# Third chunk: heads 4 to 7 first, transposed by DMA; later landing times for queries and keys in the plan; new priorities

## The chip, the cores and the metric

The kernel runs on one core of a Trainium2 chip. The metric is the device time of one execution in microseconds (us). Nine executions are given by their median. One more execution was recorded by the hardware profiler, and every row of a profile below comes from that one.

## The reference

An attention layer is followed by a gated feed-forward layer. Attention has 4 batches, 8 heads, 768 positions and 64 dimensions per head. Heads 0, 2 and 6 are "retrieval" heads with the full causal mask. The other five are "streaming" heads: a query sees the first 4 positions (the sinks) and the last 64.

```python
scores = scale * np.matmul(q, k.transpose(0, 1, 3, 2))
mask   = causal                                   # heads 0, 2, 6
mask   = causal & (pos_k < 4 | (q - k) < 64)      # the others
a      = softmax(np.where(mask, scores, -1e9))
x      = np.matmul(a, v)        # to [3072 tokens, 512]

g, val = x @ w_gate, x @ w_val  # 512 -> 1536
ffn    = (gelu(g) * val) @ w_out
out    = x + sigmoid(x @ w_res) * ffn
```

## The kernel before, in words

The 3072 tokens are cut into six chunks of 512 tokens (`CHUNKS`, numbered 0 to 5; each is four tiles of 128 tokens, and chunk 2, the third, is batch 1, tiles 2 to 5). A chunk goes through attention, then the gate and value products (L1111, twelve feature blocks `f`, each with 4 matmuls for the gate and 4 for the value), then the residual gate (L1141) and the output product (L1156). Attention of chunk c+1 is woven into the output products of chunk c.

Heads are worked in four pairs, `PAIRS = ((0, 2), (4, 6), (1, 3), (5, 7))`. A chunk runs over the pairs in `ORDER = (0, 2, 1, 3)` or in `LATER = (1, 3, 0, 2)`. `ORDER` takes heads 0, 2, 1, 3 first; `LATER` takes heads 4, 6, 5, 7 first. For each pair there are scores (L852), exponentials on ScalarE (L868), a mask on VectorE (L904), the products with the values (L976, L986, L1000), and a division (L1041, L1043). Sink scores are at L943. The normalised rows, in 16 bits, sit in `x16`; the feed-forward products need them with features on partitions, in `xT`. That transposition has two forms:

- `to_features`: TensorE transposes (L1065, four per feature block), then a copy out of PSUM on VectorE or ScalarE (L1072), one for each of the pair's two feature blocks.
- `to_features_dma`: one DMA transpose issued by SyncE (L1056) for both feature blocks.

Which form is used is decided in `attention`:

```python
if c >= DT_FIRST and P.p == order[1]:
    to_features_dma(c, P.heads[0] // 2, P.pr, x16, xdeps, xtbuf, xttoks)
```

and the order of the pairs by `order = ORDER if c < DT_FIRST else LATER`. So `DT_FIRST` sets both.

Queries and keys of chunks 0 and 1 are loaded as rows (`loads_rows`) and transposed on TensorE (L676). From chunk 2 on, `loads_natural` loads each tile in two halves (L553, issued by GpSimd, which also converts to 16 bits), and SyncE issues a DMA transpose for each tile (L717, `dT`) into `qkt`. When all eight tiles of a segment are there, SyncE issues a copy of one head's half to other partitions (L725, `q6`), which part of the scores of pair (4, 6) reads.

No order is written out by hand. Every piece of work is a `Task` with an engine, a planned duration and a priority. `Graph.schedule` plays the tasks through in planned time, and each engine's instructions are then emitted in the order that this plan gave. `Task.late` adds to the planned landing time of a DMA. It reaches no instruction by itself. `HINTS` replaces the priorities of single tasks, by task number. While TensorE has nothing to do at the start, the plan fills it with matmuls on a blank tile (L1173). On the chip each engine and each queue goes strictly through its own list, and waits are semaphores.

Of the kernel before, what the change touches and what calls it, by code (L numbers as in the profile page):

```python
# [36 lines left out]

LATER = (1, 3, 0, 2)
ROWS_UNTIL = 2
DT_FIRST = 3  # L40
DT_ALL = 9

VK = ((1, 4), (3, 4), (4, 5), (4, 7))


HINTS = (
    "0:598.78 2:-98.96 3:-24.27 16:511.03 398:-226.32 399:-81.95 400:-169.98 401:-133.18 406:592.76 "
    "428:669.65 590:-107.97 595:554.03 604:-62.97 609:119.02 611:508 631:-103.87 632:500.02 635:591.25 "
    "640:113.91 642:197.51 643:485.34 648:497.6 649:608.77 687:-2618.72 693:998.98 695:-156.54 696:-101.5 "
    "699:-194.37 703:460.62 704:468.99 706:91.16 707:1.21 708:-184.02 711:-2906.86 712:108.67 715:-113.61 "  # L50
    "722:-93.98 726:593.8 732:539.67 737:-3080.99 740:2426.17 743:-43.63 744:44.98 750:-84.74 755:-61.77 "
    "756:-226.32 757:-68.07 758:-100.39 762:-75.67 767:1467.66 783:2538.51 789:1088.69 791:2362.89 "
    "794:489.79 834:-1953.13 885:2499.66 897:2409.44 903:1361.62 910:1573 915:1075.62 921:1094.44 "
    "927:1527.46 933:2646.2 934:3345.41 946:3583 960:3450.9 963:1467.39 982:1981.84 984:1548.12 1014:3374.09 "
    "1025:2486.39 1037:3491.83 1060:2046.57 1061:2453.27 1067:3409.97 1068:1990.02 1069:3494.45 1076:2552.54 "
    "1081:2446.96 1082:3477.51 1099:2162.67 1105:3505.94 1111:3490.47 1117:3067.67 1144:3026.33 1146:3134.85 "
    "1150:118.46 1155:3543.75 1198:3516.67 1304:980.83 1313:4066.75 1341:4517.9 1343:4508.61 1358:985.12 "
    "1363:4003.98 1364:4417.91 1375:5441.35 1388:4117.01 1418:5399.99 1424:4517.89 1429:3494.32 1435:5479.84 "
    "1436:5423.25 1563:5565.33 1567:6542.91 1598:5535.71 1608:2079.98 1609:4991.07 1610:5503.31 1622:2043.57 "
    "1623:5529.25 1628:5543.06 1629:5543.02 1635:6420.01 1659:7430.01 1672:7417.77 1684:7455.84 "  # L60
)

class Task:
# [396 lines left out]
def build_kernel(nc, q, k, v, w_gate, w_val, w_out, w_res, out):  # L460
    assert N_SINK <= 64 and WINDOW == 64
    G = Graph(nc)
# [16 lines left out]
    P_vk = Pool(many("vk", 2, [128, 8, DHEAD + 1], FP16))  # L479
# [21 lines left out]
    def at(buf):  # L501
        if buf.pool is P_ps:
            return psum[:, buf.slot[0] * 512:(buf.slot[-1] + 1) * 512]
        return buf.pool.items[buf.slot]

    def at16(buf):
        return at(buf).bitcast(FP16)
# [17 lines left out]
    t_blank = G.add("dve", 0.1, lambda e: e.memset(blank[:, :], 0.0), [], -99, name="blank")  # L525
# [17 lines left out]
    t_win = t_win0 + [spread(("dve",), 600, m_win[:, 5:7, :], m_win[:, 1:2, :].to_broadcast([128, 2, 128]), 256, t_win),  # L543
                      spread(("dve",), 600, m_win[:, 0, :], m_win[:, 1, :], 128, t_win)]
    for i, vk in enumerate(P_vk.items):
        P_vk.last[i] = [G.add("dve", 0.3, (lambda vk=vk: lambda e: e.memset(vk[:, :, :], 0.0))(), [], -94, name="vzero")]
    for i, va in enumerate(P_v.items):
        P_v.last[i] = [G.add("dve", 0.15, (lambda va=va: lambda e: e.memset(va[:, :, :, DHEAD:DHEAD + 1], 1.0))(),
                             [], -95, name="vones")]

    def dma(eng, prio, cost, out_ap, in_ap, bufs=(), deps=(), name="ld", grp=None):
        issue = 0.85 if eng == "pool" else 1.2
# [93 lines left out]
    def loads_rows(c, si, b, a, z):  # L646

        n = z - a
        BB = batch(b)
        st = Buf(P_st)  # L650
        lo, hi = a * 128, z * 128
        base = {0: -60, 1: -15, 2: 50}[c]
        groups = ((0, 4), (4, 8)) if c == 0 else ((0, 8),)
        tok = {}

        def sv(j, h0, h1, w):
            return at(st)[:, :].rearrange("p (j h w) -> p j h w", j=2, h=NHEAD)[:, j, h0:h1, 0:w]
        for gi, (h0, h1) in enumerate(groups):
            for j, src in enumerate((q, k)):
                t = dma("pool", base + 4 * gi + j, (h1 - h0) * n * 0.089,  # L660
                        (lambda j=j, h0=h0, h1=h1: lambda: sv(j, h0, h1, n * 64))(),
                        src[b, h0:h1, lo:hi, :].rearrange("h (p j) d -> p h (j d)", j=n), bufs=[st])
                for h in range(h0, h1):
                    tok[j, h] = t
        values(b, a, z, base + (10 if c == 0 else 2), False, c == 0)

        per = 1 if c == 0 or n == 4 else 2
        for k_ in range(0, NPAIR, per):
            ps_ = ORDER[k_:k_ + per]
            pr = 1000 * c - 492 + ps_[0] if c else 40 * k_ - 205  # L670
            for js in (((1,), (0,)) if c == 0 else ((0, 1),)):
                scr = Buf(P_ps, "scr" if c else "scr0")
                items = [(p, jj) for jj in js for p in ps_]

                def tr(e, items=items, scr=scr):
                    return [e.transpose(out=at16(scr)[64 * x:64 * x + 64, (m * n + i) * 128:(m * n + i + 1) * 128],  # L676
                                        in_=at(st)[:, (jj * NHEAD + h) * 256 + i * 64:(jj * NHEAD + h) * 256 + (i + 1) * 64],
                                        identity=ident[:, :])
                            for m, (p, jj) in enumerate(items) for i in range(n) for x, h in enumerate(PAIRS[p])]
                tt = G.add("pe", c_mm(128, n) * len(items), tr, [t_ident] + [tok[jj, h] for p, jj in items for h in PAIRS[p]],  # L680
                           pr, bufs=[st, scr], name="qkT")
                tt.mode = "col"


                def ev(on, p0=ps_[0], scr=scr, j0=js[0], m=len(items)):
                    def fn(e):
                        o = at(BB.qkt)[:, :, :, lo:hi].rearrange("c j (y x) w -> c x (j y) w", x=2)[:, p0 % 2]
                        m0 = j0 * 2 + p0 // 2
                        o = o[:, m0:m0 + m, :].rearrange("c m (p j) -> c m p j", j=n)
                        i_ = at16(scr)[:, 0:m * n * 128].rearrange("c (m j p) -> c m p j", m=m, j=n)  # L690
                        return e.tensor_copy(out=o, in_=i_) if on == "dve" else e.activation(out=o, in_=i_, func=AF.Copy)
                    return fn
                w = n * 128 * len(items)
                t = G.flex({"dve": (c_dve(w), ev("dve")), "act": (c_act(w), ev("act"))}, [tt], pr,
                           bufs=[scr, BB.qkt], name="qkE")
                for p, jj in items:
                    for i in range(a, z):
                        (BB.ktok if jj else BB.qtok)[p, i] = t

    def loads_natural(c, si, b, a, z):  # L700

        n = z - a
        BB = batch(b)
        st = Buf(P_st)
        base = -15 if c == 1 else 1000 * (c - 2) + 50
        if BB.q6 is None:
            BB.q6 = Buf(P_q6)
        loaded = []
        for i in range(a, z):
            for j, src in ((1, k), (0, q)):  # L710
                def sv(i=i, j=j):
                    return at(st)[:, (j * 4 + i - a) * 512:(j * 4 + i - a + 1) * 512]
                ds = [dma("pool", base, 0.45,
                          (lambda sv=sv, o=o: lambda: sv().rearrange("p (o h d) -> p o h d", o=2, h=4)[:, o, :, :])(),
                          src[b, :, i * 128:(i + 1) * 128, :].rearrange("(h o) p d -> o p h d", o=2)[o], bufs=[st],
                          grp=("ld", b, i, j)) for o in range(2)]
                t = G.add("sp", 1.65, (lambda sv=sv, i=i, j=j: lambda e: e.dma_start(  # L717
                    at(BB.qkt)[:, j, :, i * 128:(i + 1) * 128], sv(), transpose=True))(), ds, base, bufs=[st, BB.qkt], dma=0.6, name="dT")
                t.late = 3.0
                loaded.append(t)  # L720
                for p in range(NPAIR):
                    (BB.ktok if j else BB.qtok)[p, i] = t
            if i == a:
                values(b, a, z, base, False)
        t = G.add("sp", 0.8, lambda e: e.dma_start(at(BB.q6)[0:64, :, a * 128:z * 128], at(BB.qkt)[64:128, :, 1, a * 128:z * 128]),  # L725
                  loaded, base + 1, bufs=[BB.qkt, BB.q6], dma=0.4, name="q6")
        t.late = 2.0
        for i in range(a, z):
            BB.q6tok[0, i] = BB.q6tok[1, i] = t
# [6 lines left out]
    def attention(c, segs, xbuf, xtbuf, xtoks, xttoks, l0=0, last=(), ek=None):  # L736
# [4 lines left out]
        todo = []  # L741
        order = ORDER if c < DT_FIRST else LATER
        for k_, p in enumerate(order):
# [54 lines left out]
        for P in todo:  # L798
# [4 lines left out]
            if P.heads[0] % 2 == 1:  # L803
                if c >= DT_FIRST and P.p == order[1]:
                    to_features_dma(c, P.heads[0] // 2, P.pr, x16, xdeps, xtbuf, xttoks)
# [467 lines left out]
```

The softmax here doesn't subtract the row's maximum and nothing guards it: scores larger than these inputs give would overflow.

## Time and profile before

| | us |
|---|---|
| median of 9 executions (lowest, highest) | 271.95 (270.97, 272.6) |
| the profiled execution | 271.83 |
| its span in the profile | 270.0 |
| TensorE (PE) busy in the span | 263.7 |
| VectorE (DVE) busy | 141.1 |
| ScalarE (ACT) busy | 139.6 |
| GpSimd (POOL) busy | 87.0 |
| first matmul that is not a filler | 6.05 |
| last matmul ends | 267.1 |

Between the span and the time of the same execution lie 1.83 us. A row of the chain or of a timeline has the start, the length, the engine and the source line. The clock granted to TensorE is 1.00 in every stretch of this profile. A matmul's row tells more by the distance from its start to the next one's start than by its own length, because neighbours overlap.

### The profile page before, as it was taken

How to read it: one execution, taken by the hardware profiler on the slowest of the kernel's cores; microseconds unless marked ns; L12 is line 12 of the kernel's file. 1: busy time of each engine (PE TensorE's matmuls, PEld its weight loads, DVE VectorE, ACT ScalarE, POOL GpSimd, SP SyncE). 2: the span in 40 equal slices, each digit the busy share in tenths (PEclk: the TensorE clock that was granted, in tenths of full speed). 3: DMA queues.
4: the chain of work that ended last, by engine and by line, in shares of the span. 5: the costliest groups of instructions: out<-in, count | busy, mean ns of one | idle time of the engine just before them, and what ended most of it. 6: DMA issues, size and time to landing. Idle time of an engine off the chain costs nothing.

```text
span 270.0 us, 5686 instructions
## 1 busy us (share of the span) xinstructions
PE 263.7 (98%) x2392; PEld 138.6 (51%) x2392; DVE 141.1 (52%) x275; ACT 139.6 (52%) x215; POOL 87.0 (32%) x124
## 2 busy tenths in 40 slices
PE   6999999999999999999999999999999999999995
PEld 5778554465444455444445444455444455444444
DVE  1798235388344456535377533376444376444344
ACT  2685456864235877333884233876333778053300
POOL 8999409995653038992000000000000000000000
DMA  6999999999999999999964100013100015100013
GB/s 82 169 206 207 186 179 229 170 162 172 177 180 148 152 154 215 149 182 169 184 124 117 41 0 0 2 41 94 65 0 0 2 39 80 66 16 0 0 39 119
DMA packets 96506, 29.12 MB, mean 108 GB/s; under 512 B 84448, under 2 KB 92896, under 8 KB 96480
## 3 DMA queue, kind: packets, MB, share of 16 engines
q0 software_dynamic: 70320, 14.69, 65.2%
q1 hardware_dynamic: 26160, 14.07, 27.7%
q8 instruction: 19, 0.31, 0.5%
q14 instruction: 7, 0.06, 0.1%
HBM read 29.36 MB, written 6.29 MB: 132 GB/s over the span
## 4 chain that ended last, share of the span: by engine, by line
PE 85%; DMA 6%; POOL 6%; issue 1%; DVE 1%; POOLq 0%; DVEq 0%
PE ps L1111 41%; PE ps L1156 23%; PE ps L1141 8%; DMA qks<-in_k_dram 6%; PE ps L852 4%; PE ps L986 3%; POOL qks L553 2%; PE ps L976 2%; PE ps L1000 1%; PE ps L1065 1%; POOL va L553 1%; POOL wv L553 1%; PE ps L676 1%; PE ps L943 1%; POOL wg L553 1%
## 5 line engine op out<-in xcount | busy, mean ns | idle before, releaser
L1125 DVE SCALAR_TENSOR_TENSOR hT<-gact,ps 128x512 f16<-128x512 f16 x68 | 45.7, 687 | 62.0 <-ACT gact L1123 34.0
L1123 ACT ACTIVATE gact<-ps 128x512 f16<-128x512 f32 x68 | 40.2, 597 | 73.3 <-PE ps L1111 71.9
L1111 PE MATMUL ps<-xT,wv 128*128 128x512 f16 x272 | 74.6, 380 | 0.0
L1111 PE MATMUL ps<-xT,wg 128*128 128x512 f16 x272 | 74.1, 380 | 0.0
L1156 PE MATMUL ps<-wo,hT 128*128 128x512 f16 (+2 forms) x312 | 70.8, 363 | 0.0
L1111 PEld LDWEIGHTS ps<-xT,wv 128*128 128x128 f16 x272 | 26.3, 98 | 31.2 <-DVE hT L1125 0.4
L1111 PEld LDWEIGHTS ps<-xT,wg 128*128 128x128 f16 x272 | 26.3, 98 | 30.5 <-ACT xT L1072 0.6
L1156 PEld LDWEIGHTS ps<-wo,hT 128*128 128x128 f16 x312 | 27.1, 97 | 26.2 <-issue 0.9
L553 POOL DMA_DIRECT2D qks<-in_k_dram x36 | 28.7, 836 | 32.0 <-DMA qkt<-qks 22.2
L868 ACT ACTIVATE er<-ps 128x1024 f16<-128x1024 f32 (+4 forms) x40 | 34.2, 891 | 7.5 <-PE ps L852 7.3
L553 POOL DMA_DIRECT2D qks<-in_q_dram x36 | 28.8, 849 | 0.8 <-DVE ident L526 0.8
L1160 DVE SCALAR_TENSOR_TENSOR otile<-srs,ps 128x512 f32<-128x512 f32 (+2 forms) x26 | 16.7, 644 | 17.4 <-PE ps L1156 17.2
L1141 PE MATMUL ps<-wr,xT 128*128 128x512 f16 x96 | 24.5, 380 | 0.0
L553 POOL DMA_DIRECT2D va<-in_v_dram x24 | 21.5, 940 | 3.0 <-PE ps L1000 3.0
L1144 ACT ACTIVATE srs<-ps 128x512 f32<-128x512 f32 x24 | 14.3, 597 | 13.6 <-PE ps L1141 13.6
L1163 DVE TENSOR_TENSOR otile<-otile,xtok 128x512 f32<-128x512 f32 (+2 forms) x26 | 16.8, 647 | 0.7
L1043 DVE TENSOR_TENSOR xtok<-ps,rcp 128x512 f32<-128x512 f32 (+1 forms) x28 | 16.9, 609 | 0.5
L852 PE MATMUL ps<-qkt 64*128 64x64 f16 (+3 forms) x391 | 17.0, 213 | 0.1
L852 PEld LDWEIGHTS ps<-qkt 64*128 64x128 f16 x391 | 9.9, 95 | 9.1 <-issue 4.7
L868 ACT ACTIVATE es<-ps 128x1024 f16<-128x1024 f32 (+1 forms) x14 | 12.6, 900 | 3.2 <-PE ps L852 3.2
L1141 PEld LDWEIGHTS ps<-wr,xT 128*128 128x128 f16 x96 | 8.5, 97 | 9.6 <-issue 0.6
L1173 PE MATMUL ps<-blank 128*128 128x128 f16 x109 | 10.8, 248 | 2.6 <-DVE blank L525 2.6
(69 smaller groups left out, 215.4 us busy)
## 6 DMA issues: line engine op xcount, KB each, us to landing
out_dram<-otile SPq DMA_DIRECT2D x23, 256.0 KB, 2.1
va<-in_v_dram POOLq DMA_DIRECT2D x24, 128.0 KB, 18.0
qks<-in_k_dram POOLq DMA_DIRECT2D x32, 64.0 KB, 12.8
qks<-in_q_dram POOLq DMA_DIRECT2D x32, 64.0 KB, 13.2
wg<-in_moe_w_gate_dram POOLq DMA_DIRECT2D x3, 512.0 KB, 10.4
wv<-in_moe_w_val_dram POOLq DMA_DIRECT2D x3, 512.0 KB, 10.8
wo<-in_moe_w_out_dram POOLq DMA_DIRECT2D x4, 384.0 KB, 23.1
vs<-va SPq DMA_DIRECT2D x4, 260.0 KB, 6.7
```

The lines of the kernel that those rows point to most:

```text
L553: return G.add(eng, issue, lambda e: e.dma_start(out_ap(), in_ap), deps, prio, bufs=bufs, dma=cost, name=name, grp=grp)
L852: return [e.matmul(at(scr)[:, oo:oo + w], lhsT=side(BB, low, 1)[half, k0:k0 + 128], rhs=side(BB, low, 0)[half, qq:qq + w], start=True, sto ...
L868: return e.activation(out=o, in_=i_, func=AF.Exp, scale=SM_SCALE)
L1043: t2 = G.add("dve", c_dve(2 * n * 64), lambda e: e.tensor_tensor(out=xview(), in0=avv(0, DHEAD), in1=scale(), op=ALU.mult), [t1] + xdeps, ...
L1111: return lambda e: [e.matmul(at(dst)[:, :], lhsT=w[:, ci, f * 128:(f + 1) * 128], rhs=at(xtbuf)[:, ci, :], start=(ci == 0), stop=(ci == NC ...
L1123: ta = G.add("act", c_act(512), (lambda gb=gb, ga=ga: lambda e: e.activation(out=at(ga)[:, :], in_=at(gb)[:, :], func=AF.Gelu))(), [tg], p ...
L1125: th = G.add("dve", c_dve(512), (lambda vb=vb, ga=ga, f=f: lambda e: e.scalar_tensor_tensor(out=at(h)[:, f, :], in0=at(ga)[:, :], scalar=0 ...
L1141: e.matmul(at(rb)[:, :], lhsT=at(xtbuf)[:, ci, s], rhs=wr[:, ci, :], start=(ci == 0), stop=(ci == NCB - 1))
L1144: ta = G.add("act", c_act(512), (lambda rb=rb, sr=sr: lambda e: e.activation(out=at(sr)[:, :], in_=at(rb)[:, :], func=AF.Tanh, scale=0.5)) ...
L1156: e.matmul(at(fb)[:, w], lhsT=at(h)[:, fi, s], rhs=wo[:, fi, w], start=(fi == 0), stop=(fi == NF - 1))
L1160: t1 = G.add("dve", c_dve(n), (lambda fb=fb, sr=sr, ot=ot, w=w: lambda e: e.scalar_tensor_tensor(out=at(ot)[:, w], in0=at(sr)[:, w], scala ...
L1163: t2 = G.add("dve", c_dve(n), (lambda ot=ot, lt=lt, w=w: lambda e: e.tensor_tensor(out=at(ot)[:, w], in0=at(ot)[:, w], in1=at(xbuf)[:, lt, ...
```

## The change

Four edits, with one new table of priorities.

- `DT_FIRST` goes from 3 to 2. Chunk 2 takes the pairs in the order `LATER`, and its second pair's `x16` (heads 4 to 7) is transposed by one DMA on SyncE instead of by eight TensorE transposes with two copies.
- The planned landing of the row loads of chunk 1 is 1.2 us later (`t.late`), and that of all natural loads of queries and keys 5.0 us later.
- The two kinds of constant fill on VectorE (`vzero`, `vones`) come after the fill of the blank tile.
- `HINTS` is a different table, so that the order of instructions differs on every engine.

```diff
-DT_FIRST = 3
+DT_FIRST = 2
 DT_ALL = 9
...
 HINTS = (
-    "0:598.78 2:-98.96 3:-24.27 16:511.03 398:-226.32 399:-81.95 400:-169.98 401:-133.18 406:592.76 "
...
+    "0:-96.05 3:-32.5 13:-14.98 398:-205.14 399:-3161.01 400:-242.48 401:-60.67 406:194.11 428:585.68 "
...
     for i, vk in enumerate(P_vk.items):
-        P_vk.last[i] = [G.add("dve", 0.3, (lambda vk=vk: lambda e: e.memset(vk[:, :, :], 0.0))(), [], -94, name="vzero")]
+        P_vk.last[i] = [G.add("dve", 0.5, (lambda vk=vk: lambda e: e.memset(vk[:, :, :], 0.0))(), [t_blank], -94, name="vzero")]
     for i, va in enumerate(P_v.items):
         P_v.last[i] = [G.add("dve", 0.15, (lambda va=va: lambda e: e.memset(va[:, :, :, DHEAD:DHEAD + 1], 1.0))(),
-                             [], -95, name="vones")]
+                             [t_blank], -95, name="vones")]
...
                         src[b, h0:h1, lo:hi, :].rearrange("h (p j) d -> p h (j d)", j=n), bufs=[st])
+                t.late = 1.2 if c else 0.0
...
                           grp=("ld", b, i, j)) for o in range(2)]
+                for d in ds:
+                    d.late = 5.0
```

What the built programs show of it: TensorE has 64 transposes of `x16` in place of 72. After the fillers, all other kinds of matmul are there in equal numbers. From the first 128x512 gate matmul to the end, both programs change the array's tiling mode 82 times. Before that point, the fillers after the second block of transposes are 74 in place of 78, and the fillers ahead of the first transposes 42 in place of 31. GpSimd issues the first keys' load directly after the first queries' load, with the select for `ident` behind both, and the list of loads is otherwise the same up to the second half of the loads for chunk 3. SyncE has one entry more.

## The prediction

> **What bounds the kernel now.** I read the page's busy times and slices first, then the waits of TensorE, then the chain that ended last, then timelines of the places that the change touches.
>
> ```profile
> PE 263.7 (98%) x2392; PEld 138.6 (51%) x2392; DVE 141.1 (52%) x275; ACT 139.6 (52%) x215; POOL 87.0 (32%) x124
> ...
> PE   6999999999999999999999999999999999999995
> ...
> DMA  6999999999999999999964100013100015100013
> ```
>
> TensorE (PE) is busy in every slice; the DMA engines are full for half the span. So the question for every edit is whether it takes work from PE, or makes PE wait. The waits, in total, times, longest:
>
> ```profile
> PE ps L1173 <- DVE blank L525: 2.6, 1, 2.6
> PE ps L676 <- DMA qks<-in_k_dram: 0.5, 1, 0.5
> ```
>
> Only two, both ahead of 8.1 us. A third is too short for that view, and stands in the chain:
>
> ```profile
> 18.67 17.42 DMA qks<-in_k_dram
> 36.09 0.14 issue
> 36.22 0.64 PE ps L676 x16
> ```
>
> The last keys of chunk 1 land at 36.09. The four 128x256 matmuls before began at 35.48, at 0.1085 each (start to start) end at 35.91, and a change of tiling mode adds 0.095: PE could have gone on at 36.01, so it lost 0.21. From there to 264.5 PE shows no idle time. What is taken from PE there comes off the end, and nothing else does.
>
> Now the transposes that go, in chunk 2:
>
> ```profile
> 102.93 0.39 PE L1065 MATMUL ps<-ident,x 128*128 128x128 f16 x4
> 103.15 1.03 PE L1141 MATMUL ps<-wr,xT 128*128 128x512 f16 x4
> ```
>
> Four take 0.22 from their start to the next one's start. The second four follow at 104.02.
>
> Last, SyncE's queue (SPq), where the replacement goes:
>
> ```profile
> 76.70 0.66 SPq L725 DMA_DIRECT2D q<-qkt  x1
> 77.40 15.66 SPq L717 DMA_TRANSPOSE qkt<-qks  x5
> 93.19 1.15 SPq L636 DMA_DIRECT2D vs<-va  x2
> 94.48 3.85 SPq L717 DMA_TRANSPOSE qkt<-qks  x3
> 98.73 0.62 SPq L725 DMA_DIRECT2D q<-qkt  x1
> 99.41 2.06 SPq L717 DMA_TRANSPOSE qkt<-qks  x1
> ```
>
> It is nearly always occupied or blocked by a wait for loads (15.66 us for five). The answers for three lines give the landing after issue, min/median/max: the q6 copy (L725), the transposes of loads between 60 and 100 us (L717), and the transpose of x16 (L1056), which today runs only after 141 us, with DMA quiet:
>
> ```profile
> DMA to landing us min/median/max: 2.5/6.9/8.4
> ...
> DMA to landing us min/median/max: 6.1/8.0/9.3
> ...
> DMA to landing us min/median/max: 3.0/3.1/4.1
> ```
>
> **What the Trainium skill says.** "TensorEngine Tiling (Array Packing)", Key Properties, says a change of tiling mode drains TensorE. The trace agrees: a 128x512 matmul takes 0.2165, and 0.31 when the mode changes after it. "Perfetto Trace Analysis", Tensor Engine Instruction, says that a matmul's end is estimated; so I use distances between starts. "DMA: Bandwidth & Descriptors", Queues, rings and completion order, says that a DMA engine goes round robin between queue rows. This agrees with SyncE's transposes needing 6.1 to 9.3 while GpSimd's row is full. "Advanced Engine Details and Errata", X-Bar Transpose, says a transpose DMA is as fast as a plain one; in quiet 3.1 against the 2.1 of a 256 KB output, so only roughly.
>
> **The change, part by part.**
>
> *Later landing times.* They are numbers of the plan and cost nothing themselves. GpSimd's list of loads stays, except that four value loads go 1.5 loads earlier. What they do is move consumers.
>
> *Transposes.* Eight leave PE: 2 x 0.22 = 0.44. Two copies out of PSUM leave ScalarE or VectorE (0.60 or 0.42 each), worth nothing: both idle near half the time. The other matmuls from the first 128x512 gate matmul on are equal in kind and number, and there are 82 mode changes in both programs. Summing the distances between starts over both lists gives 240.79 and 240.35: the same 0.44.
>
> *The keys' wait.* Between the first 128x512 gate matmul (25.51) and chunk 1's first transposes, 32 of width 512 and 32 of width 256 stand now (6.93 + 3.47 = 10.4); after, 42 and 24 (9.09 + 2.60 = 11.7). The transposes come 1.3 later, at about 37.3, and the load has landed: -0.21. But the third piece of the gate weights, landed at 27.90 and asked for at 28.55 now, is asked for earlier: the list puts only 8 matmuls of width 512 and 4 of 256 between 25.51 and it (1.73 + 0.43), so at 27.68. A new wait of 0.22. Bounds 0 to 0.25; I take 0.15, since an earlier keys' load moves the queue up a little.
>
> *The head.* The second block of transposes waits for the first keys (landed 7.98). Their issue moves from 2.53 to about 2.2, past one select (0.30). The landing gains 0 to 0.35, as the transfer's own share is not visible; I take 0.15. Behind it PE's list up to the first 128x512 matmul sums to 17.25 before (17.49 measured) and 17.36 after, a difference of +0.1 covered by that slack: zero. The fill order on VectorE starts the fillers about 1.3 earlier with 11 more of them: nothing.
>
> *q6 for chunk 2.* Pair (4, 6) moves from third to first, so its copy, landed at 85.15 and read at 97.64 now, is read right after the sink scores (86.4) and 12 matmuls: 86.4 + 0.3 + 2.6 + 0.1 = 89.4, less the 0.3 gained ahead: 89.1. On SyncE it now stands behind twelve load transposes instead of eleven, and behind chunk 0's fourth output, whose last products moved to about 73.4 on PE. Its two VectorE operations queue each behind a gate-times-value operation that comes every 1.73 (eight matmuls): ready at 77 to 78, where 70.62 was. Then one transpose (1.3 median, 2.6 longest) and the copy at 79.3 to 80.7. Landing 6.9 to 8.4 later: 86.2 to 89.1. Slack 0 to 2.9, cost taken 0.
>
> *The new DMA transpose of x16.* SyncE's entries ahead of it include all those of the last fence. That puts it at 102 to 103.3. What stands behind it (a copy of values, chunk 1's outputs, the load transposes for chunk 4) comes its 1.24 later, and PE reads none of that before 170. Its data are ready before: the second pair's products end near 98.4, and the division takes 0.69 on VectorE. Landing: 3.1 from below (quiet), 9.3 from above (longest under load); I take 6.6, the median of load transposes issued from 96 to 110: 108.6 to 109.9. By the distances between starts summed over its list, PE reaches chunk 2's first gate product near 108.2 (none is woven into the attention any more, as six were at 106.1 to 108.1); the list gives twelve matmuls (2.6) that read heads 0 to 3 alone: needed at 110.8. Slack 0.9 to 2.2, cost taken 0; at the upper bound 112.6 a wait of 1.8.
>
> Sum: -0.44 - 0.21 + 0.15 - 0.15 = **-0.65**. Against the profiled execution 271.83 that is 271.18; its own time lies 0.12 under the median, so against the median I forecast **271.3**.
>
> **The rivals.**
>
> *Gain eaten, no change (27%).* The head gives nothing and the weights' wait costs its full 0.25: -0.44 - 0.21 + 0.25 = -0.40, and one wait of 0.1 for an exponential in the reordered chunks makes it -0.3: 271.65. For it: VectorE and ScalarE get new orders in five chunks. Against it: PE waited for neither by more than 0.2 in the old ones.
>
> *Slower by the DMA transpose (25%).* The x16 transpose has two times the data of a load transpose and sits in SyncE's in-order queue at a time when DMA is full. If it lands later than 112.0, PE's wait of 1.2 turns the sum positive by over 0.5, for PE's list has nothing else to do. At the upper bound of 112.6 it is 1.8 - 0.65 = +1.15: 273.1. For it: the wait is new and its cover only 2.6 us of matmuls. Against it: every transpose issued from 96 to 110 landed within 7.0.
>
> *The change doesn't do what it says.* The loads themselves hardly move; that is in the forecast already, since no gain is booked for them.
>
> **How the numbers follow.** A measurement of this kernel can tell about 0.2% (0.54 us) from no change. The likeliest case (48%) is 271.3; its own range is 270.9, with the full 0.35 at the head and no wait for weights, to 271.45. The second is 271.65, the third 272.5 to 273.1. The range of 270.7 to 272.7 leaves out the late half of the third case and little below. Faster by over 0.2% 0.48, within 0.27, slower 0.25.
>
> **What would show it.** In the profile after: 64 matmuls at the transposes' line; no wait at chunk 1's first transposes, one of about 0.2 at the third gate weights near 27.7; the first q6 copy landed before 89; SyncE's first transpose of x16 issued near 102 to 103 and landed before 110.8; PE without idle time from 38 on. It is wrong if PE waits for the x16 transpose or the q6 copy at all by more than 0.5, if the last matmul starts less than 0.4 or more than 1.1 earlier than 266.9, or if VectorE or ScalarE shows up among PE's releasers with more than 0.3.

## The result, and the profile after

The changed kernel takes **270.56 us** (median of 17 executions, 270.37 to 271.21). Run beside it, the kernel before took 272.35 (54 executions, 270.97 to 272.74). The ratio is **0.9946, with a 95% interval of 0.9936 to 0.9956**. A later measurement gave 270.6 against 272.25, and 0.9946 again (0.9929 to 0.9963). The forecast was 271.3 with a range of 270.7 to 272.7: the sign was right, the size less than half of what came, and 270.56 lies just under the range.

The profiled execution took 270.42 with a span of 268.7, against 271.83 and 270.0. From the page, the busy times:

```profile
PE 264.6 (98%) x2391; PEld 139.0 (52%) x2391; DVE 140.6 (52%) x273; ACT 139.8 (52%) x215; POOL 87.1 (32%) x124
```

TensorE's busy time has grown by 0.9, though 8 transposes left: 11 more fillers run ahead of the first transposes. Busy time is no measure of progress here. The waits of TensorE (in total, times, longest):

```profile
PE ps L1178 <- DVE blank L527: 1.1, 1, 1.1
```

The wait for the first keys is gone from the view. What limits TensorE early is in the chain that ended last:

```profile
14.61 12.45 DMA wg<-in_moe_w_gate_dram
27.06 0.05 issue
27.11 1.47 PE ps L1116 x6
```

Before, the last load in the chain was that of chunk 1's keys (landed 36.09). Now it is the third piece of the gate weights, landed at 27.06; TensorE goes on at 27.11, 0.22 after it could have. Chunk 1's keys landed at 35.41 and are read at 36.73. After 27.1 the chain has no other load. TensorE's timeline at the gate stage of chunk 2, and its last batch of output products:

```profile
106.38 0.61 PE L1070 MATMUL ps<-ident,x 128*128 128x128 f16 x8
106.83 1.02 PE L1161 MATMUL ps<-wo,hT 128*128 128x512 f16 x4
107.69 1.02 PE L1116 MATMUL ps<-xT,wg 128*128 128x512 f16 x4
...
110.28 0.59 PE L1116 MATMUL ps<-xT,wg 128*128 128x512 f16 x2
...
263.00 2.81 PE L1161 MATMUL ps<-wo,hT 128*128 128x256 f16 x36
```

The product at 110.28 is the first that needs the half transposed by DMA. The last batch starts at 263.00; before it was this row:

```profile
264.30 2.81 PE L1156 MATMUL ps<-wo,hT 128*128 128x256 f16 x36
```

So the pair of traces differs by 1.30 there, which is the whole difference of the spans. SyncE's queue after:

```profile
80.04 0.67 SPq L730 DMA_DIRECT2D q<-qkt  x1
...
102.25 1.38 SPq L1061 DMA_TRANSPOSE xT<-x  x1
```

From issue to landing the copy of q6 took 6.6, and the transpose of `x16` this:

```profile
DMA to landing us min/median/max: 7.6/7.6/7.6
```

It landed at 109.86, and TensorE wanted it at 110.28: 0.42 to spare. The margin differs from trace to trace: 0.36 in the second trace of the changed kernel, and between 0.04 (e8) and 1.51 (e12) in the experiments below that keep its order behind chunk 1.

### The profile page after: what moved, and what is told of

The parts are those of the page before. It is cut to its first block, busy times and chain, and to the rows that moved or that the text cites. A ratio compares the mean times of both kernels' runs of the same rounds, so it can differ in the third digit from the quotient of the medians.

```text
span 268.7 us, 5676 instructions
## 1 busy us (share of the span) xinstructions
PE 264.6 (98%) x2391; PEld 139.0 (52%) x2391; DVE 140.6 (52%) x273; ACT 139.8 (52%) x215; POOL 87.1 (32%) x124
## 4 chain that ended last, share of the span: by engine, by line
PE 88%; DMA 5%; POOL 2%; DVE 1%; issue 0%; DVEq 0%
PE ps L1116 43%; PE ps L1161 23%; PE ps L1146 8%; DMA wg<-in_moe_w_gate_dram 5%; PE ps L857 4%; PE ps L991 3%; PE ps L981 2%; PE ps L1005 1%; PE ps L1098 1%; PE ps L1070 1%; PE ps L679 1%; PE ps L948 1%; POOL wg L555 1%; POOL wv L555 1%; POOL vk L603 0%; DVE otile L1168 0%
## 5 line engine op out<-in xcount | busy, mean ns | idle before, releaser
L1161 PEld LDWEIGHTS ps<-wo,hT 128*128 128x128 f16 x312 | 27.4, 98 | 27.1 <-issue 0.7
L857 PE MATMUL ps<-qkt 64*128 64x64 f16 (+4 forms) x391 | 16.9, 213 | 0.0
L1178 PE MATMUL ps<-blank 128*128 128x128 f16 x116 | 11.7, 254 | 1.1 <-DVE blank L527 1.1
```

The lines of the kernel that those rows point to most:

```text
L857: return [e.matmul(at(scr)[:, oo:oo + w], lhsT=side(BB, low, 1)[half, k0:k0 + 128], rhs=side(BB, low, 0)[half, qq:qq + w], start=True, sto ...
L1161: e.matmul(at(fb)[:, w], lhsT=at(h)[:, fi, s], rhs=wo[:, fi, w], start=(fi == 0), stop=(fi == NF - 1))
```

## The experiments

Most edits move single tasks in the finished plan. `put(x, y)` takes task x out of its engine's list and puts it ahead of y. The task numbers are the planner's. All ratios are to the kernel before, run beside it: e1 to e4 on one chip, e5 to e8 on a second, e9 to e12 on a third. Of these sets only the last has the changed kernel itself (e11), so a comparison of e3 to e8 with it is one across chips.

### Is it the head?

In the pair of traces the first keys landed 1.08 earlier, for an issue 0.34 earlier, and the first 128x512 gate product started 0.79 earlier. I therefore thought at first that the head had given most of the gain.

```diff
# e1: before
     span = G.schedule()
+    put(first_keys_load, select_for_ident)
# e2: before, the same and
+    put(fill_of_blank, first_task_on_VectorE)
```

> The kernel before with one instruction pair exchanged: on GpSimd the first keys' load is issued ahead of the select that makes the identity; every other order is that of before. My theory (the head gives the larger part of the gain, because the first keys land about 1.1 us earlier, not 0.33): keys issued at about 2.19 and landed at about 6.9 to 7.0 instead of 7.98, TensorE's second block of transposes at about 7.56 instead of 8.02 (13 filler matmuls are then the bound), first 512-wide gate product about 0.45 to 0.55 earlier than 25.51, time -0.45 us (0.9975 to 0.9990 of before). The prediction's own step (only 0.33 earlier, most of it absorbed) would give 0 to -0.3 us. Rival (the head gains nothing to the end, since the loads of values and weights that follow land as they did): within 0.2 us of before.

> As the run with the first keys' load ahead of the select, and on VectorE the fill of the blank tile moved to the very front, so that TensorE's fillers start at about 1.1 to 1.2 instead of 2.6. My theory: the first block of transposes then begins as its load lands (5.6 to 5.7 instead of about 5.9), the second block at about 7.1 to 7.35, the first 512-wide gate product at about 24.7 as in the changed kernel, time -0.7 to -0.8 us against before (about 0.9973): two moves in the head, and nothing else of the change, give half of its gain. Rival (keys' load alone is what counts): the same as the run without the earlier fill, -0.45 us.

Measured: 0.9988 (0.9976 to 1.0001) and 1.0003 (0.9984 to 1.0021). In both traces the first keys landed at 6.92 to 6.93, and the first 128x512 gate product started at 24.75, as early as in the changed kernel. By its time, e1 lies within the 0.9975 to 0.9990 of my theory; e2, which should have gained more, gained nothing. The chains and the last batches, first of e1, then of e2:

```profile
18.80 16.72 DMA qks<-in_k_dram
35.51 0.14 issue
35.65 0.64 PE ps L676 x16
...
263.72 2.81 PE L1156 MATMUL ps<-wo,hT 128*128 128x256 f16 x36
```

```profile
18.76 17.01 DMA qks<-in_k_dram
35.77 0.14 issue
35.90 0.64 PE ps L676 x16
...
263.97 2.81 PE L1156 MATMUL ps<-wo,hT 128*128 128x256 f16 x36
```

TensorE came earlier to the transposes of chunk 1, and waited 0.32 and 0.52 for their keys. The start of the last batch against that landing: before, 264.30 - 36.09 = 228.21; with the keys first 263.72 - 35.51 = 228.21; with both 263.97 - 35.77 = 228.20. **In these three traces the end hangs on the landing of chunk 1's last keys, whatever the head does.** My theory of the head fell with this: the first gate product is 0.75 earlier in both traces, the end 0.58 and 0.33, as much as the keys landed earlier.

The other direction, in the changed kernel:

```diff
# e3: after
     span = G.schedule()
+    put(select_for_ident, first_keys_load)
```

> The changed kernel with one exchange undone: on GpSimd the select of the identity stands again ahead of the first keys' load. My theory: keys land at about 7.9 to 8.0 again, second transposes at about 8.0, everything behind them 0.6 to 0.75 us later than in the changed kernel, so 271.1 to 271.3, -1.0 to -1.2 us against before become -0.7 to -0.9 (ratio about 0.997). Rival (the head's gain came from elsewhere, or is absorbed by 24.7): same time as the changed kernel, 0.9946.

Measured 271.13 and 0.9973 (0.9963 to 0.9984). By the time, the expectation is met; by the mechanism, not. The first keys were issued at 2.53 and landed at 7.02, not 7.9. The second transposes came at 7.73 because the fillers ahead of them took longer: the matmuls started 0.106 apart until 7.1, and 0.056 apart behind that, where the changed kernel's first trace goes over to 0.056 at about 6.2. (The profile gives the granted clock as 1.00 for these stretches in every trace, so it doesn't show this, before either.) The chain has no first keys in it, but this:

```profile
14.67 13.30 DMA wg<-in_moe_w_gate_dram
27.96 0.05 issue
28.01 1.47 PE ps L1116 x6
...
263.91 2.81 PE L1161 MATMUL ps<-wo,hT 128*128 128x256 f16 x36
```

Its last batch starts at 263.91, and 263.91 - 27.96 = 235.95. The changed kernel has 263.00 - 27.06 = 235.94, and its second trace 263.17 - 27.23 = 235.94:

> The changed kernel once more, on the chip of these runs, as the measure for the other three and for the kernels made from it: 270.4 to 271.2 us, ratio 0.994 to 0.997, no run above 271.8 us. In the trace, if the third piece of gate weights lands behind 26.85, the last matmul starts 238.53 us behind that landing (27.06 and 265.59 in the first trace; 27.96 and 266.50 with the select first).

(270.6, 0.9946; the last matmul of all starts 238.53 behind the landing, as expected.) So the changed kernel's end hangs on the third gate weights as the old one's does on the keys.

Both are in one list of loads. In twelve of the fourteen traces the keys landed 8.34 to 8.40 behind the weights; in the other two 8.19 and 8.25. At equal landings the changed kernel ends its list at keys + 235.94 - 8.35 = keys + 227.59, the old one at keys + 228.21. **That is a gain of 0.62 at equal landings**, for the usual spacing of these two loads. (The kernel before had 8.19 in its own trace; set against its third gate weights, at 27.90, its end is 0.46 behind that of the changed kernel.) The other 0.68 of the pair's 1.30 is that the same load landed at 35.41 instead of 36.09.

### The eight transposes

```diff
# e10: before, half of chunk 2's transposes left out
+    gone = [both TensorE transposes of 4, and their two copies]
```

> The kernel before without the 8 matmuls that transpose the second half of chunk 2's x on TensorE and without their two copies; nothing takes their place, so that half of chunk 2's features is not computed (its gate products read what the buffer held). Theory: these 8 transposes cost TensorE 0.44 us and hide nothing, so the last matmul starts 230.36 us behind the landing of chunk 1's keys instead of 230.80, spread as in before, ratio 0.9984. Rival (they stood in time in which TensorE would have waited for ScalarE, VectorE or a psum buffer): 0 to -0.2 us, and a wait of TensorE shows in their place. Rival on the other side (their copies delayed others on VectorE and ScalarE too): more than -0.6 us.

The half left out is, unlike the expectation says, that of heads 0 to 3, the two blocks of four at 102.93 and 104.02 in the trace before; number and kind are those of the other half. Measured 271.8, 0.9996 (0.9985 to 1.0006). Its chain and its last batch:

```profile
18.74 17.42 DMA qks<-in_k_dram
36.16 0.14 issue
36.30 0.64 PE ps L676 x16
```

```profile
264.06 2.81 PE L1156 MATMUL ps<-wo,hT 128*128 128x256 f16 x36
```

264.06 - 36.16 = 227.90: leaving them out gains **0.31** in this trace, not 0.44. The median alone wouldn't have shown it; 0.31 is 0.11%, within the interval. The two programs' matmuls, set side by side from the keys' landing on, show where the other 0.13 goes. Behind the first four, the program without them is ahead by 0.22, as expected. Behind the second four it is ahead by 0.31 and not by 0.44, for TensorE now waits there, too shortly for the list of its waits. The row of its weight load shows it:

```profile
104.10 0.11 PEld L976 LDWEIGHTS ps<-vs,er 128*64 128x64 f16 x1 [0.56 <-DVE xtok L1043]
```

The products with the values (L976) could have begun at 103.96 (one product of 0.2165 and a change of mode of 0.095 behind 103.65). They begin at 104.10, behind a division on VectorE that ends at 104.04. So the price of 0.44 was right, and 0.13 of it covered a wait for VectorE, which is the expectation's first rival in part.

Then the changed kernel with TensorE doing chunk 2 again:

```diff
# e5: after
     (in HINTS the task numbers from 1036 on raised by 3)
...
-            if c >= DT_FIRST and P.p == order[1]:
+            if c > DT_FIRST and P.p == order[1]:
```

> The changed kernel with chunk 2's second half of x transposed by TensorE again (8 transposes, in three psum tiles with their copies) and its heads in the old order; loads, head and all else as in the changed kernel. Theory: the 8 transposes are worth their own time with both changes of TensorE's mode, 0.44 us, so this kernel takes 0.35 to 0.5 us more than the changed one (ratio to before 0.9960 to 0.9965). Rival (the transposes were hidden, gain lies wholly in the head): within 0.1 us of the changed kernel. Second rival (the DMA transpose lands only just in time and costs a hidden wait): the kernel without it is faster than the changed one.

Measured 272.98, 1.0038 (1.0024 to 1.0053): 2.4 above the changed kernel, five times what was expected. Its waits:

```profile
PE ps L1116 <- DVE xT L1077: 0.6, 1, 0.6
...
PE ps L1146 <- ACT gact L1128: 0.3, 1, 0.3
PE ps L1070 <- DVE x L1046: 0.3, 1, 0.3
```

They stand at 109.04 to 110.25 and 132.22. The plan, laid out anew, has the last transposes directly ahead of the first gate products, so a chain of norm, transpose and copy lies open at the border of two stages. In the changed kernel four output products lie between them (106.83). That these waits belong to the layout and not to the eight transposes is shown by the next kernel, which has the DMA transpose. So e5 doesn't price the transposes.

```diff
# e6: after
-                t.late = 1.2 if c else 0.0
...
-                for d in ds:
-                    d.late = 5.0
```

> The changed kernel without the two planned landing times (queries and keys booked at their bare landing time, as before), same order numbers otherwise; the planner then lays out another order on every engine. Theory (the planned landing times book nothing on the chip; they only steer the planner, and what counts is whether TensorE meets a load that has not landed): time within 0.4 us of the changed kernel, and any excess shows as waits of TensorE for DMA or for another engine in chunk 1's or chunk 2's first scores and transposes. Rival (landing times are what removes the waits of chunk 1): the wait for chunk 1's keys at about 35.9 is there again with 0.2 us or more, and others with it, +0.4 to +1 us.

Measured 273.25, 1.0051 (1.0037 to 1.0065). Its waits:

```profile
PE ps L1113 <- DVE xT L1074: 0.6, 1, 0.6
...
PE ps L1143 <- ACT gact L1125: 0.3, 1, 0.3
PE ps L1067 <- DVE x L1043: 0.3, 1, 0.3
```

The same three waits of 0.6, 0.3 and 0.3, at the same places, and behind the head two others, of 0.3 for values (14.11) and 0.6 for an exponential (50.09). The rival's wait for chunk 1's keys isn't among them. Both kernels keep priorities that were set for another plan, so they show what it costs when the table no longer fits the plan, 2.4 and 2.7 us, and not what the planned landing times are worth with a table of their own. That wasn't tried.

### The DMA transpose's margin

```diff
# e7: after
+    put(x16_transpose_by_DMA, the_entry_behind_the_next_copy_and_store)
```

> The changed kernel with the DMA transpose of chunk 2's x put behind two other transfers on SyncE's queue (a shift of values and a store), so issued at about 104 to 105.3 instead of 102.25; nothing else moved. It took 7.6 us to land, at 109.86, and TensorE wanted it at 110.28, a slack of 0.42. Theory (slack is gone at once): it lands at 111.5 to 113 and TensorE waits 1.2 to 2.6 us for it, time about 1.2 to 2.6 us above the changed kernel: level with before or slower (271.7 to 273.1). Rival (its latency is queueing behind transfers that end anyway, so it lands at about the same time): at most 0.5 us above the changed kernel. Second rival (other gate products that are ready fill the wait in part): in order issue forbids it, so none of it is expected.

Measured 273.01, 1.0039 (1.0019 to 1.0059); the runs scatter more than others (270.9 to 277.4). It was issued at 104.73, 2.48 later, and landed 8.0 later at 112.77. In its waits of TensorE:

```profile
PE ps L1116 <- DMA xT<-x: 2.3, 1, 2.3
```

The landing came 2.91 later, TensorE reached the product 0.23 later (110.51), the margin took 0.42, and the rest is this wait. The slower rival of the prediction was two places in a queue away.

The wait is not the whole price. The last matmul starts 4.23 later than in the changed kernel's trace. Of this, 0.23 is there already and 2.30 is the wait. The other 1.70 is lost directly behind it, where products of width 512 start 0.43 apart instead of 0.2165. By stretch, the busy time of TensorE, its matmuls, the granted clock, and the share and rate of the DMA engines:

```profile
113.00:116.00 3.00, 3.00 (x8) 0.50 1.63 200
```

The clock granted to TensorE was 0.50 from 112.98 to 116.39; no other trace shows a clock below 1.00 between the head and the end. Of the 22 executions, the seven with a mean clock of 0.994 or less are the seven longest (274.45 and more); the others took at most 273.64. So the scatter goes with that lower clock, though only one of them was traced.

### Waits removed one at a time

```diff
# e4: after
+    put(gate_product_of_block_11, behind_those_of_blocks_8_and_7)
# e8: after
+    put(second_queries_load, select_for_ident); put(second_keys_load, select_for_ident)
+    (7 of the 13 fillers between the first and second transposes left out)
+    (the edit of e4)
```

> The changed kernel with one matmul moved on TensorE: the second product of the first half of chunk 0 that reads the third piece of gate weights (landed 27.06, wanted at 26.85) goes behind two others that need pieces already there. Theory: the wait of 0.225 us at 26.7 to 27.1 goes, and nothing takes its place; time 0.2 us below the changed kernel (ratio to before about 0.9939 instead of 0.9946). Rival (wait is only moved: the next product or its value partner waits for the fourth piece, or the GELU behind it is late): no change against the changed kernel, within 0.1 us.

> The changed kernel with three edits in the head: the select of the identity behind all four first loads on GpSimd; 7 of the 13 filler matmuls between the first and the second block of transposes left out; the product that waits for the third piece of gate weights moved behind two others. Fillers compute nothing that is used. Theory: the second keys' and queries' loads land about 0.3 us earlier, the second block of transposes starts at about 6.95 (the keys' landing at 6.9) instead of 7.32, and the whole gains 0.2 to 0.6 us over the changed kernel (ratio about 0.993). Rival (the blocks behind are bound by their own loads, at 8.76 and 10.15, or the select then comes too late for the first transposes at 5.7): no gain, or up to 0.4 us slower.

Measured 0.9965 (0.9953 to 0.9977) and 0.9990 (0.9973 to 1.0008): neither beats the changed kernel. But the edit of e4 does not take the wait away. It moves a product of feature block 11 behind one of block 8 and one of block 7, and block 8 reads the third piece of the gate weights too (`wtok["g", f // 4]`: blocks 8 to 11). So one of the "two others that need pieces already there" needs the same piece, and TensorE asks for it at the same place of its list. The row of the first weight load there names it still:

```profile
27.13 0.99 PEld L1116 LDWEIGHTS ps<-xT,wg 128*128 128x128 f16 x6 [0.37 <-DMA wg<-in_moe_w_gate_dram]
```

The wait is short in this trace, 0.07 on the matmuls, because the piece landed at 26.97 and TensorE came only at 27.09, and it may be one for ScalarE, on which the product waits too (27.03). TensorE had been held up before, and the chain starts there:

```profile
3.26 5.60 DMA qks<-in_q_dram
```

That is the second queries, landed at 8.86, with TensorE idle 0.34 ahead of the third transposes. In e8, TensorE waits 0.23 for the first keys, 0.71 for the second queries (9.19) and 0.20 for values (13.80). These loads are all near enough to being the bound that a wait can stand at another of them. What it would gain to take the weights' wait away was not measured.

Why e8 loses 1.1 on the changed kernel in its median is not settled: its trace starts the last batch only 0.6 later. In that trace the DMA transpose of `x16` lands at 110.86 and is read at 110.90, with 0.04 to spare, and the two longest of its 14 executions (273.49 and 276.17) show the two lowest clocks (0.992 and 0.994). Some of them may have waited there as e7 does; none that did was traced.

### The keys' slack, both ways

The kernel before has two groups of times: of 174 executions in the four comparisons, 98 lie below 272.2, around 271.6, and 76 above it, around 272.5. Of 66 executions in the changed order (the changed kernel twice, e3, e4 and e12), none is above 272.2; of e8's 14, two are, those with the low clock. Does the upper group come from the wait for chunk 1's keys?

```diff
# e9: before, on TensorE and ScalarE
-    [chunk 1's first 16 transposes], [gate products x4]
+    [gate products x4], [chunk 1's first 16 transposes]
# e12: after
+    put(chunk_1_first_16_transposes, three_gate_tasks_earlier)
```

> The kernel before with one move in chunk 0's gate stage: TensorE's first block of chunk 1's transposes (16, which need the last of chunk 1's keys) goes behind two gate tasks that are ready (0.87 us of 512-wide products), and ScalarE's copy of its result behind the GELU of those. Three traces with this order (before: keys landed 36.09, last matmul 266.90; keys first: 35.51 and 266.31; keys and fill first: 35.77 and 266.56) have the last matmul 230.80 us behind the keys' landing, within 0.02. Theory now (that landing, not TensorE's head, sets the end of before, and varies by up to 1.3 us from run to run): with 0.65 us of slack the wait is gone, the runs above 272.2 us that make up a third to a half of before's mostly vanish, median 0.4 to 0.9 us below before (ratio 0.9967 to 0.9985). Rival (before's spread comes from something later in the kernel; the wait is only what the trace shows, 0.2 us): -0.2 us at most, the same spread as before.

> The changed kernel with the first block of chunk 1's transposes moved ahead of three ready gate tasks (1.3 us), so that TensorE wants chunk 1's keys at about 35.4 instead of 36.7, as early against their landing as in the kernel before. Theory (the keys' slack, which the planned later landing gave, is what the median gained beyond the transposes): the last matmul starts about 230.2 us behind that landing whenever it waits, the spread of before comes back (270.5 to 272.2), median 0.4 to 0.9 us above the changed kernel on this chip. Rival (slack is worth only the 0.2 us of the trace): within 0.25 us of the changed kernel.

Measured: e9 271.46 against 272.25, 0.9985 (0.9971 to 0.9999), with 2 of 12 above 272.2 where before had 17 of 34 on that chip. Its list of waits of TensorE has no load, only the fillers' and one of 0.2 for VectorE. So slack for the keys gives the old kernel about 0.4 by the ratio. The small share above 272.2 need not come from the slack: e1, which has none, has 2 of 14, where before had 20 of 51 on its chip (e2 has 6 of 14). e12 took 271.17, 0.9960 (0.9947 to 0.9974): 0.57 above the changed kernel, within what was expected, but its times (270.74 to 271.27) show no upper group. It waited for the weights (27.57), and its last batch starts 236.32 behind that landing, 0.38 more than in the changed kernel. Two waits too short for the list make this up: 0.17 for chunk 1's keys, which landed at 35.97 and are read at 36.11, and 0.21 for ScalarE at 38.63. So the keys' wait was there again, but small. The two runs don't agree on the upper group. **Where it comes from stays open**: no trace fell into it.

## Why the prediction was right, and where not

The direction was right, and so is most of what it said of the profile; the size was less than half. In the pair of traces, the way from the first 128x512 gate product to the last matmul takes 241.38 before and 240.87 after. That is -0.51, where the terms for this part (-0.44, -0.21 and +0.15) sum to -0.50. The rest of the pair's 1.30, 0.79, is an earlier first gate product, for which the head's -0.15 stood.

- **The transposes (-0.44).** Right in price: the distances between starts give 0.44. In the order of before, leaving them out gains 0.31, as 0.13 of them covered a wait for VectorE.
- **The keys' wait (-0.21) and the weights' wait (+0.15).** Both as said: the first is gone, the second stands there with 0.22, the value worked out before it was shaded. What doesn't hold is to book them as amounts that stay the same in every execution. Each ties the end to the landing of one load. At equal landings, trading one tie for the other, with all else but the transposes, was worth 0.62 - 0.44 = 0.18, or 0.31 with the transposes at 0.31. What taking the new wait away would bring was not measured, since e4 leaves it in place.
- **The head (-0.15).** This is the term that was mis-sized. "The landing gains 0 to 0.35" was too low for the landing itself: the first keys gained 1.08 in the pair (7.98 to 6.90), for 0.34 at the issue. And the gain was thought to end where that load's cover ends, while the end hangs on later loads of the same list. Chunk 1's keys landed at 36.04 in the mean of the four traces with the old issue (35.62 to 36.30), and at 35.72 in the mean of the nine with the new one and no other load moved (35.32 to 36.32). The difference of 0.32 is the 0.33 of the issue, but the scatter is as large. By times, undoing the exchange (e3) costs 0.9973 against 0.9946, or 0.45 to 0.73 us, but across chips; on e3's own chip e4, which has the new issue, has a mean of 270.87 against e3's 271.09, 0.22 less. The same exchange in the kernel before gave 0.12% in e1 and nothing in e2. So some gain through the later loads is likely, and its size isn't shown.
- **"Its own time lies 0.12 under the median"**, so the sum was carried from one execution to a median. With two groups of times that is weak ground. That the sum of -0.65 lies close to the 0.62 at equal landings is luck: the head's -0.15 is not part of that measure, and the other terms sum to -0.50. Of the medians' 1.65 to 1.79, 0.62 is what equal landings give, about 0.3 more may come from earlier loads, and the rest, some 0.8, goes with the upper group that is gone. Before's lower group alone has its median at 271.63, 1.0 above the changed kernel. The mark set beforehand, more than 1.1 at the last matmul, was passed by 0.2 (266.90 to 265.59).
- **q6.** Issue 79.3 to 80.7, landing 86.2 to 89.1, wanted at 89.1: it was 80.04, 86.60 and 88.73. Right.
- **The transpose of `x16`.** Issue 102 to 103.3, landing 108.6 to 109.9, wanted at 110.8: it was 102.25, 109.86 and 110.28. Right, with 0.42 to spare instead of 0.9 to 2.2. The load transposes on which the 6.6 rested had half its data; it took 7.6 and, when moved, 8.0. That it shares the DMA engines with GpSimd's full row, as the Trainium skill has it in "DMA: Bandwidth & Descriptors" (Queues, rings and completion order), fits: later, in quiet, it took 3.1 to 4.7.
- **The rivals.** "Slower by the DMA transpose" has its mechanism shown in e7, where the landing of 112.77 made the kernel slower by 0.39%. There the prediction priced the wait too low: a wait of 2.3 cost 4.0 in the trace, as the clock was 0.50 for 3.4 us behind it. "Gain eaten" did not come: the terms behind the head came out near their forecast, and the first gate product started 0.79 earlier instead of at the same time.

## What to carry over

Where TensorE follows a row of loads closely, don't add up its waits: find which landing the end hangs on, by the constant distance from it to the last work over several traces, and ask which landing would be next. Compare two kernels at equal landings as well as by their times; here this parted 0.62 from what varies with the loads. When a kernel without some work gains less than that work's price, set its matmuls beside the old ones: a wait too short for the list of waits can be what took the place, as the 0.13 in e10. And when an experiment is meant to remove a wait, find in its trace the place where the wait stood: in e4 the next product asked for the same load.

## What the hardware showed that was not expected

- One list of loads, issued at the same times to within 0.3 us from the fifth load on, landed its last keys of chunk 1 anywhere from 35.32 to 36.32, with the extra time at a different load in each trace: 3.4 between the first gate and the first value weights in e3 (16.97 to 20.33), 3.5 ahead of the third gate weights in e5 (24.47 to 27.98), where 2.5 is usual. What causes it no run shows.
- With the old issue of the first keys (2.52 to 2.53) they landed at 7.75, 7.98 and 8.02 in three traces and at 7.02 in the fourth. With the issue at 2.19 to 2.20 they landed at 6.89 to 6.96 in all ten. So 0.33 at the issue moved this landing by about 1 in most traces, and yet chunk 1's keys differ by only 0.32 in the mean.
- Behind a pause of TensorE of 2.3 us in the middle of the kernel, the granted clock was 0.50 for 3.4 us (e7), which cost 1.7 us on top of the pause. That the pause brought it about fits the one trace, and isn't shown by an experiment of its own.
